# Loads of weight chunks moved from ScalarE's queue to SyncE's, and the start of their rounding tied to a count of products

## The chip, the cores and the metric

The kernel runs on one core of a Trainium2 chip. The metric is the device time of one execution in microseconds; the time before is the median of 7 runs. Engines are named as in the profile: PE (matmul), DVE (VectorE), ACT (ScalarE), POOL (GpSimd) and SP (SyncE, which here only issues DMAs). ACT can issue DMAs too.

## The reference

The output of a retention block feeds a gated feed-forward block:

```python
# q, k, v: (8, 8, 576, 64) float32, D = 64
scores = q @ k.T / sqrt(D)
ret    = scores * Dmat                 # gamma_h ** (i - j) for i >= j, else 0
x      = (ret @ v)                     # (B, H, S, D) -> (4608, 512)
xn     = x / sqrt(mean(x * x) + 1e-6) * rms_g
g, val = xn @ w_gate, xn @ w_val       # (512, 1536) each
out    = (g * sigmoid(g) * val) @ w_out  # (1536, 512)
```

The three weight matrices come as float64 and all else as float32.

## The kernel before

**Stages.** The 4608 tokens are 12 units of 384. The retention part is cut into jobs: one pair of heads of one batch (batch 1 is cut in two). Jobs 0 to 7 run first, on data loaded at the start; they give the tokens of units 0 and 1. Then come the up products of these two units (`up_plain`, line 640): for each third g of the columns, gate (m = 0) and then value (m = 1), units 0 and 1, four products each, 48 in all. A product is four matmuls of 128x384, which the trace shows as eight records; gate products are evicted by ACT (SiLU, L660), value products by DVE (L658). Jobs 8 to 11 are dealt with between these products. After that the output products of units 1 and 0 run (`across`, line 712), and then units 2 to 11 with a seven-product (Strassen) scheme for both matrices, about 950 us in which weights are already there.

**Weights.** The float64 words are rounded to float32 by the kernel. The weights are 18 chunks of 1 MB of words (lines 821 to 833): 0 to 11 for gate and value, in the order in which the up products use them, 12 to 17 for w_out. A chunk i goes through these steps:

- `load_chunk` (L855) loads its words into one of four places, `spare(i)`. A place is free when the mantissa of the chunk that was there is done. Chunks 12 to 17 have the places 1, 2, 3, 2, 3, 3; places 0 to 2 are in w_out, so chunk 17 waits for the mantissa of 16, and 16 for that of 14.
- `exponent` (DVE L871) takes the exponents out of the words; three activations on ACT (L887) turn them into scale factors. They are put in a list `acts` and issued one by one with `act()`.
- `mantissa` (DVE L898, L903, L908) makes the number without its exponent. L908 needs the last of the three activations.
- `join` (DVE L916) multiplies both.

The generator `rounding()` (line 932) puts these steps in order: exponent of i, if it was not taken ahead; exponent of i + 1, if it is loaded; mantissa of i; loads up to chunk i + 5, where a place is free; exponent of i + 1 if not yet; join of i. From chunk 4 on these loads are issued by ACT. The loop over the up products (line 1041) takes two steps of the generator behind each product (`weights(2)`), and as many as are needed at once where a product cannot go on without a chunk (`weights_to`). 

**Order.** There is no scheduler: each engine runs its instructions in the order in which the code records them, and so does each queue's issue of DMAs. An instruction that waits holds back what is behind it on its engine. Each DMA uses one of eight semaphores in turn, whichever engine issues it, and is not issued before the previous DMA with its semaphore has landed.

**Jobs among the products.** At steps 29, 33, 37 and 41 of the up products `later` calls `slot(j)` for jobs 8 to 11; at 45 the rest of job 11 follows. A slot lets PE finish the previous job (`values`, L390; `carried`, L412) and make the scores and states of this one (L307, L329); DVE weighs the scores (L342), writes x (L435, which frees the two banks of `values`) and sums the states (L366). `following(j)` then transposes job j + 1 on DVE (L272, from qraw and kraw) and scales its v on ACT (L285), and SP loads job j + 2 in 13 DMAs (qraw and kraw four each, L156; k and v two each, L224; vt, L229). The first of them waits for the transpose, since qraw has one buffer. PE has five banks of PSUM that products and slots take in turn.

After the last chunk `combine_out` (L690) makes four sums of blocks of w_out on DVE, which the output products use.

Of the kernel before, what the change touches and what calls it, by code (L numbers as in the profile page):

```python
# [35 lines left out]
def _causal_table():  # L36

    return np.ascontiguousarray(np.tile(np.triu(np.ones((L, L), np.float32)), (2, 1)))
# [3 lines left out]
def kernel(  # L42
# [11 lines left out]
    nc = tc.nc  # L54
# [776 lines left out]
    for f in range(0, NF, 2):  # L831
        chunks.append((w_out[:, f : f + 2], moe_w_out, slice(f * P, f * P + 2 * P), slice(None)))
    LATER = (1, 2, 3, 2, 3, 3)
    words_of, exp_of, waits_at = {}, {}, {}
    n_chunks = n_loads = 0

    free = w_up[0][:, 8:].rearrange("p b f -> p (b f)")
# [1 line left out]
    def spare(i):  # L839

        return i % 4 if i < n_up else LATER[i - n_up]

    def load_chunk(i, queue):
        dst, src, rws, cols = chunks[i]
        if src.dtype != F32:
            n = dst.shape[1]
            cols = slice(2 * (cols.start or 0), 2 * cols.stop if cols.stop else None)
            src = src.bitcast(U32)
            at = spare(i)
            dst = free[:, : 4 * DM] if at == 3 else (  # L850
                w_out[:, 4 * at : 4 * at + 4].rearrange("p c f -> p (c f)")
            )
            dst = words_of[i] = dst.bitcast(U32).rearrange("p (c f) -> p c f", c=n)
            waits_at[at] = i
        queue.dma_start(out=dst, in_=src[rws, cols].rearrange("(c p) f -> p c f", p=P))  # L855

    def load_chunks(n, queue=nc.scalar):

        nonlocal n_loads
        while n_loads < min(n, len(chunks)) and waits_at.get(spare(n_loads)) is None:  # L860
            load_chunk(n_loads, queue)
            n_loads += 1

    def exponent(i):

        if i not in words_of:
            return
        at = (4 + i % 2 * 2) * DM
        e = free[:, at : at + 2 * DM].bitcast(U32)
        e = e.rearrange("p (c f) -> p c f", c=chunks[i][0].shape[1])  # L870
        nc.vector.tensor_scalar(  # L871
            out=e, in0=words_of[i][..., 1::2], scalar1=20, scalar2=0x7FF,
            op0=ALU.logical_shift_right, op1=ALU.bitwise_and,
        )
        f = e.bitcast(F32)
        acts.extend((
            (i, dict(out=f, in_=e, bias=least)), (i, dict(out=f, in_=f, bias=most, scale=-1.0)),
            (i, dict(out=e, in_=f, bias=top, scale=-(2.0**23))),
        ))
        exp_of[i] = e  # L880
# [32 lines left out]
    def join(i):  # L913
        if i in words_of:
            dst = chunks[i][0]
            nc.vector.scalar_tensor_tensor(  # L916
                out=dst, in0=dst, scalar=2.0**-20, in1=exp_of.pop(i).bitcast(F32),
                op0=ALU.mult, op1=ALU.mult,
            )
            del words_of[i]  # L920
# [11 lines left out]
    def rounding():  # L932

        nonlocal n_chunks
        for i in range(len(chunks)):
            if i not in exp_of and i in words_of:
                exponent(i)
                yield
            for ahead in (True, False):
                if i + 1 in words_of and i + 1 not in exp_of and i > (1 if ahead else 0):  # L940
                    exponent(i + 1)
                    yield
                if ahead:
                    yield from mantissa(i)
                    load_chunks(i + 5 if i else 0)
                    yield
            join(i)
            n_chunks += 1
            yield
# [8 lines left out]

    def weights_to(n):

        while n_chunks < min(n, len(chunks)):
            next(steps)

    def start():

        h_of[0] = ffn.tile([P, NF, U], F32, tag="h", name="h_0")
        tables = list(zip((causal, gv, gc, gq, gx), (_causal_table(), *_decay_tables(H, D))))

        def table(i, queue):
            t, values_ = tables[i]
            src = nc.inline_tensor(values_, name=t.tensor.name + "_table")
            queue.dma_start(out=t, in_=src.ap())

        make_identity(nc, ident)
        nc.scalar.activation(out=tick, in_=mhalf[:1], func=AF.Silu)
        nc.vector.memset(ones, 1.0)
        warm = bank("warm")
        for _ in range(6):  # L980
            nc.tensor.matmul(warm[:, :P], lhsT=ones, rhs=ones, start=True, stop=True)
        first_places.update(find_places())
        load_chunks(1)
        for i in (1, 0, 2):
            table(i, nc.scalar)
        weights(3)
        for j in range(2 * NHP):
            load_first(j, {0: range(2), 1: range(2, H)}.get(j))
            if j == 1:
                table(3, nc.sync)  # L990
            load_chunks((1, 1, 1, 1, 2, 2, 2, 3)[j], nc.sync)
        table(4, nc.sync)
        nc.sync.dma_start(out=rms_g, in_=moe_rms_g.rearrange("(c p) -> p c", p=P))
        load_chunks(4, nc.sync)
        turn(0)
        scale_v(0)
        act(3)
        squares = []

        def later(step):  # L1000

            if step == LATER_AT[0] - 8:
                following(2 * NHP - 1)
            elif step in LATER_AT:
                j = 2 * NHP + LATER_AT.index(step)
                if j < LATER_JOBS:
                    slot(j, rest=(j > 2 * NHP))
                    if j + 1 < LATER_JOBS:
                        following(j)
                else:  # L1010
                    values(j - 1)
                    carried(j - 1)

        for j in range(2 * NHP):
            slot(j)
            if j + 1 < 2 * NHP:
                turn(j + 1)
            if squares:
                gather(*squares.pop())
            for i in ((1,), (2,), (3,), (4, 5), (6,), (7,), (), ())[j]:  # L1020
                scale_v(i)
            if j:
                u, c = divmod(j - 1, NHP)
                squares.append((u, c, square(u, c)))
            act(1)
            if j == 5:
                norm_1(0)
            elif j == 6:
                norm_2(0)
            weights((2, 0, 0, 1, 1, 1, 1, 0)[j])  # L1030
            if j == 4:
                gather(*squares.pop())
            elif j == 5:
                diagonals(0)
            act(1)
        gather(*squares.pop())
        load_qk(2 * NHP)
        load_kv(2 * NHP)
        made = combine_out()
        step = -1  # L1040
        for m, g in [(m, g) for g in range(NG) for m in range(2)]:
            for u in range(2):
                weights_to(4 * g + 2 * m + 1)
                for i, _ in enumerate(up_plain(u, m, g)):
                    step += 1
                    later(step)
                    if not (u or m or g):
                        if i == 0:
                            values(2 * NHP - 1)
                            carried(2 * NHP - 1)  # L1050
                            gather(1, NHP - 1, square(1, NHP - 1))
                        elif i == 1:
                            norm_1(1)
                        elif i == 2:
                            diagonals(1)
                        elif i == 3:
                            norm_2(1)
                    weights(2)
                    act(1)
                    if u and m and g == NG - 1:  # L1060
                        weights_to(len(chunks))
                        next(made, None)
                    if i == 1:
                        weights_to(4 * g + 2 * m + 2)
        for _ in made:
            pass
        for blk, t in first_blocks.items():
            keep(blk, t)
        rest = across(1)
        next(rest)  # L1070
        following(LATER_JOBS - 1)
        for i, _ in enumerate(rest):
            if i == 1:
                norm_0(2)
                differences(0)
            elif i == 2:
                norm_1(2)
                diagonals(2)
            elif i == 4:
                norm_2(2)  # L1080
        rest = across(0)
        next(rest)
        combine(1)
        slot(LATER_JOBS, rest=False)
        following(LATER_JOBS)
        for _ in rest:
            pass
        combine(0)
        slot(LATER_JOBS + 1)
        load_next(LATER_JOBS + 1)  # L1090
        turns.append(LATER_JOBS + 1)
# [74 lines left out]
```

## Time and profile before

| what | value |
|---|---|
| median of 7 runs | 1147.78 us (1145.84 to 1151.02) |
| profiled execution, its own time | 1145.84 us |
| its span, first to last instruction | 1144.1 us |
| PE busy | 1119.8 us, 98% |
| PEld busy | 1044.3 us, 91% |
| DVE busy | 733.6 us, 64% |
| ACT busy | 258.3 us, 23% |
| mean granted PE clock | 0.992 of full |
| chunks issued by ACT in the profile | w_out and w_gate places, 1024 KB each |

How to read it: a row of a timeline gives the start and duration in us, the engine (SPq and ACTq are the issuing of DMAs by SP and ACT), the line of the kernel, the operation, what it writes and reads, how many instructions are merged in the row, and in brackets how long the engine had been idle before and what ended that. The profile's lines are those of the kernel before; in the kernel after they are 3 higher from the middle of `load_chunk` on (2 higher at the load itself) and more behind `rounding`. The output products of unit 1 (`xo`, L726) start at 195.46 us.

### The profile page before, as it was taken

To read this page: it belongs to the slowest core of one execution; us is meant where nothing else is said; L and a number is where in the kernel's file an instruction comes from. 1 tells how busy PE (TensorE), PEld (TensorE's weight loads), DVE (VectorE), ACT (ScalarE), POOL (GpSimd) and SP (SyncE) were. 2 spreads that over 40 slices of the span, in tenths; PEclk is the share of its full clock that TensorE was granted. 3 is DMA by queue.
4 is the path that set the end of the run, shared out by engine and by line. 5 is a ranking of instruction groups with operands and counts; after the bars stand their busy time and mean duration, and the time that the engine had idled before them with its cause. 6 is when DMAs were issued, how large, how long until landed. Compare 5 with 4: busy or idle time off the path is not lost.

```text
span 1144.1 us, 24779 instructions
## 1 busy us (share of the span) xinstructions
PE 1119.8 (98%) x10454; PEld 1044.3 (91%) x10454; DVE 733.6 (64%) x1452; ACT 258.3 (23%) x508; POOL 40.1 (4%) x68
## 2 busy tenths in 40 slices
PE   7899988999999999999999999999999999999998
PEld 6655656999999999999999999999999999999998
DVE  5888878746686686376766676466577566446353
ACT  5556532102211221211221120121221221120210
POOL 0100000290000000000000000000000000000000
PEclk9899999999999999999999999999999999999999
DMA  8844556434553556044344456305436503303304
GB/s 209 225 130 146 143 133 193 90 68 116 125 128 68 150 139 158 8 102 106 97 117 76 110 139 130 118 27 121 103 95 140 132 32 94 128 1 98 124 1 111
DMA packets 307039, 126.72 MB, mean 111 GB/s; under 512 B 284528, under 2 KB 289904, under 8 KB 306928
## 3 DMA queue, kind: packets, MB, share of 16 engines
q1 hardware_dynamic: 296784, 108.98, 38.9%
q10 hardware_dynamic: 10144, 16.16, 4.4%
q8 instruction: 82, 1.34, 0.5%
q14 instruction: 29, 0.24, 0.1%
HBM read 110.14 MB, written 14.94 MB: 109 GB/s over the span
## 4 chain that ended last, share of the span: by engine, by line
PE 89%; DVE 6%; DMA 2%; issue 1%; ACT 1%; SPq 1%; POOL 0%; DVEq 0%; POOLq 0%; ACTq 0%
PE w L595 13%; PE x L595 12%; PE z L595 12%; PE up L652 9%; PE xo L726 8%; PE wo L726 8%; PE zo L726 8%; PE y L595 6%; PE yo L726 4%; PE av L390 2%; PE s L307 2%; PE av L412 1%; PE s L329 1%; DVE sum L366 1%; DVE x L435 1%
## 5 line engine op out<-in xcount | busy, mean ns | idle before, releaser
L619 ACT COPY m<-x 128x384 f32<-128x384 f32 x60 | 28.8, 479 | 338.0 <-PE x L595 338.0
L726 PE MATMUL xo<-h,w_out 128*128 128x192 f32 x528 | 90.3, 328 | 0.0
L595 PE MATMUL w<-sums,w_val 128*128 128x192 f32 x480 | 88.6, 328 | 0.4
L595 PE MATMUL x<-x,w_val 128*128 128x192 f32 x480 | 88.7, 328 | 0.0
L595 PE MATMUL x<-x,w_gate 128*128 128x192 f32 x480 | 88.7, 328 | 0.0
L595 PE MATMUL w<-sums,w_gate 128*128 128x192 f32 x480 | 87.9, 326 | 0.0
L595 PE MATMUL z<-x,w_gate 128*128 128x192 f32 x480 | 87.8, 326 | 0.0
L595 PE MATMUL z<-x,w_val 128*128 128x192 f32 x480 | 87.8, 326 | 0.0
L726 PEld LDWEIGHTS xo<-h,w_out 128*128 128x128 f32 x528 | 85.9, 190 | 0.6
L726 PE MATMUL wo<-h,w_out 128*128 128x192 f32 x504 | 85.6, 326 | 0.4 <-DVE c_last L774 0.4
L602 DVE TENSOR_TENSOR u<-m,y 128x384 f32<-128x384 f32 x60 | 33.1, 552 | 78.0 <-PE y L595 78.0
L726 PEld LDWEIGHTS wo<-h,w_out 128*128 128x128 f32 x504 | 82.4, 190 | 0.7 <-DVE c_last L774 0.7
L595 PEld LDWEIGHTS w<-sums,w_val 128*128 128x128 f32 x480 | 79.2, 190 | 2.7 <-DVE c L602 2.7
L595 PEld LDWEIGHTS x<-x,w_val 128*128 128x128 f32 x480 | 79.1, 190 | 0.6
L595 PEld LDWEIGHTS x<-x,w_gate 128*128 128x128 f32 x480 | 79.3, 190 | 0.5
L595 PEld LDWEIGHTS z<-x,w_gate 128*128 128x128 f32 x480 | 79.6, 190 | 0.0
L595 PEld LDWEIGHTS z<-x,w_val 128*128 128x128 f32 x480 | 79.6, 190 | 0.0
L595 PEld LDWEIGHTS w<-sums,w_gate 128*128 128x128 f32 x480 | 79.5, 190 | 0.1
L602 DVE TENSOR_TENSOR h<-u,w 128x384 f32<-128x384 f32 x60 | 33.0, 550 | 69.4 <-PE w L595 69.4
L652 PE MATMUL up<-x,w_gate 128*128 128x384 f32 x192 | 65.8, 499 | 4.8 <-DVE x L435 3.3
L614 ACT ACTIVATE h<-h 128x384 f32<-128x384 f32 x90 | 47.2, 524 | 88.5 <-DVE h L602 88.5
L652 PEld LDWEIGHTS up<-x,w_gate 128*128 128x128 f32 x192 | 36.6, 194 | 30.9 <-issue 5.6
(189 smaller groups left out, 1809.8 us busy)
## 6 DMA issues: line engine op xcount, KB each, us to landing
w_out<-w_blocks SPq DMA_DIRECT2D x70, 768.0 KB, 5.3
out_dram<-o SPq DMA_DIRECT2D x364, 24.0 KB, 1.6
qraw<-in_q_dram SPq DMA_DIRECT2D x96, 72.0 KB, 2.8
kraw<-in_k_dram SPq DMA_DIRECT2D x96, 72.0 KB, 2.8
k<-in_k_dram SPq DMA_DIRECT2D x48, 128.0 KB, 2.9
v<-in_v_dram SPq DMA_DIRECT2D x48, 128.0 KB, 3.0
w_out<-in_moe_w_gate_dram ACTq DMA_DIRECT2D x5, 1024.0 KB, 5.8
w_out<-in_moe_w_out_dram ACTq DMA_DIRECT2D x3, 1024.0 KB, 6.2
```

The costliest lines, as they stand in the source:

```text
L307: nc.tensor.matmul(s[side(odd), e, i * L : i * L + L], lhsT=d["kT"][side(e), c * L : c * L + L], rhs=d["qT"][side(e), c * L : c * L + L], ...
L329: nc.tensor.matmul(o[side(e)], lhsT=d["k"][side(odd), i, e], rhs=d["v"][side(odd), i, e], start=True, stop=True,)
L366: nc.vector.scalar_tensor_tensor(out=d["sum"][c], in0=d["sum"][c - 1], scalar=gc[:, hp : hp + 1], in1=part, op0=ALU.mult, op1=ALU.add,)
L390: mm = nc.tensor.matmul(av[odd][column(j, odd, e), i * L : i * L + L], lhsT=d["v"][side(odd), i, e] if c < NC - 1 else d["vt"][:, e], rhs= ...
L412: mm = nc.tensor.matmul(av[odd][column(j, odd, e), i * L : i * L + L], lhsT=d["sum"][c - 1][side(e)], rhs=d["qT"][side(e), c * L : c * L + L],
L435: nc.vector.tensor_tensor(out=x[to, first - c0 // L :: 2], in0=av[odd][at, i * L : (i + n) * L].rearrange("p (c k) -> p c k", k=L), in1=g. ...
L595: nc.tensor.matmul(ps[:, i * HU : i * HU + HU], lhsT=w_up[m][:, 2 * blk + c, cut], rhs=t_of[u][blk][:, c], start=(start and i == c == 0), ...
L602: nc.vector.tensor_tensor(out=o, in0=a, in1=pairs_of(ps), op=ALU.add)
L614: nc.scalar.activation(out=o, in_=c, func=AF.Silu)
L619: nc.scalar.copy(out=s1, in_=pairs_of(x_))
L652: nc.tensor.matmul(ps[:, :U], lhsT=w_up[m][:, 4 * half + c, i * P : i * P + P], rhs=x_of[u][:, c], start=(c == 0), stop=(c == NHP - 1),)
L726: nc.tensor.matmul(ps[:, i * HU : i * HU + HU], lhsT=a[:, c, i * P : i * P + P], rhs=rhs[:, c], start=(start and i == c == 0), stop=False, ...
```

## The change

`load_chunks` in `rounding()` is called with SP's queue, so chunks 4 to 17 are issued by SP, each at the place in SP's order where the code records it: among the loads of the jobs. For each chunk `there_at` holds the number of the product at which it was loaded, plus 3 (0 for chunks loaded before the up products), and `now` counts the products. `rounding()` takes the exponent of a chunk that is loaded only from that product on; while it waits so for the exponent of i itself, it gives its step back without work. Inside `weights_to` (`due`) the count is not asked for.

```diff
     LATER = (1, 2, 3, 2, 3, 3)
-    words_of, exp_of, waits_at = {}, {}, {}
+    words_of, exp_of, waits_at, there_at = {}, {}, {}, {}
+    now = 0
+    due = False
...
         queue.dma_start(out=dst, in_=src[rws, cols].rearrange("(c p) f -> p c f", p=P))
+        there_at[i] = now + 3 if now else 0
...
         for i in range(len(chunks)):
+            while i in words_of and i not in exp_of and not due and now < there_at[i]:
+                yield
             if i not in exp_of and i in words_of:
                 exponent(i)
                 yield
             for ahead in (True, False):
-                if i + 1 in words_of and i + 1 not in exp_of and i > (1 if ahead else 0):
+                if (
+                    i + 1 in words_of and i + 1 not in exp_of and i > (1 if ahead else 0)
+                    and (due or now >= there_at[i + 1])
+                ):
                     exponent(i + 1)
                     yield
                 if ahead:
                     yield from mantissa(i)
-                    load_chunks(i + 5 if i else 0)
+                    load_chunks(i + 5 if i else 0, nc.sync)
                     yield
...
     def weights_to(n):
 
+        nonlocal due
+        due = True
         while n_chunks < min(n, len(chunks)):
             next(steps)
+        due = False
...
-        step = -1
+        now = 0
...
                 for i, _ in enumerate(up_plain(u, m, g)):
-                    step += 1
-                    later(step)
+                    later(now)
+                    now += 1
```

In the order that the two kernels record on DVE, all steps of the rounding stand in the same places up to the mantissa of chunk 13 and the exponent of chunk 14. From there the exponent of 15 moves from before the mantissa of 14 to behind job 9's slot and the transposes of job 10; that of 16 from behind the join of 14 to behind the mantissa of 15; that of 17 from before the join of 16 to two products later, behind the first value product of unit 0. On SP, chunks 4 and 5 stand before job 8's loads, 6 to 12 behind them, 13 and 14 behind job 9's, 15 and 16 behind job 10's, and 17 behind the loads of both job 11 and job 12.

More of the change, by code (lines that the diff above doesn't have):

```diff
@@ L959, in weights_to @@
     def weights_to(n):
+        nonlocal due
+        due = True
         while n_chunks < min(n, len(chunks)):
             next(steps)
+        due = False
     def start():
+        nonlocal now
         h_of[0] = ffn.tile([P, NF, U], F32, tag="h", name="h_0")
```

## The prediction

> **What bounds the kernel now.** The page's busy line first, then the chain of waits in order of time, then the stages, then each engine's timeline where PE stood idle.
>
> ```profile
> span 1144.1 us, 24779 instructions
> PE 1119.8 (98%) x10454; PEld 1044.3 (91%) x10454; DVE 733.6 (64%) x1452; ACT 258.3 (23%) x508; POOL 40.1 (4%) x68
> ```
>
> PE is the bound: whatever the change is worth must be PE idle time or a slower PE clock. The stages (us, PE busy, PEld, DVE, ACT, POOL, granted clock, DMA share, GB/s) say where that is:
>
> ```profile
> 62.00:108.00 46.00, 45.29 (x142) 26.52 (x141) 41.00 (x48) 27.96 (x32) 0.00 (x0) 1.00 0.43 137
> 143.50:160.00 16.50, 13.21 (x86) 7.38 (x84) 15.22 (x24) 8.70 (x14) 0.00 (x0) 0.90 0.57 129
> 160.00:178.30 18.30, 14.69 (x198) 9.78 (x189) 10.88 (x21) 7.78 (x14) 0.18 (x2) 0.91 0.73 170
> 178.30:195.50 17.20, 16.88 (x97) 10.04 (x98) 13.31 (x23) 0.00 (x0) 0.09 (x1) 1.00 0.40 139
> ```
>
> While the up chunks are rounded (62 to 108) PE hardly stops. It loses time from 143.5 to 178.3, where the chunks of w_out are rounded, and the PE timeline names the three stops:
>
> ```profile
> 143.51 2.85 PE L652 MATMUL up<-x,w_gate 128*128 128x384 f32 x8
> 149.65 9.67 PE L652 MATMUL up<-x,w_gate 128*128 128x384 f32 x24 [3.29 <-DVE x L435]
> 174.09 0.70 PE L390 MATMUL av<-ret,v 64*64 64x64 f32 x16 [2.33 <-ACT w_val L660]
> 178.27 10.59 PE L652 MATMUL up<-x,w_val 128*128 128x384 f32 x32 [1.29 <-DVE h L658]
> ```
>
> Those are 6.9 us idle; behind the idle the clock was 0.90 and 0.91 of full, 1.65 us each. PE waits for DVE and ACT, and DVE in turn for loads:
>
> ```profile
> 144.41 0.69 DVE L871 TENSOR_SCALAR w_gate<-w_out 128x1024 uint32<-128x1024 uint32 x1 [4.67 <-DMA w_out<-in_moe_w_out_dram]
> 163.86 0.57 DVE L272 STREAM_TRANSPOSE qT<-qraw 128x384 f32<-128x384 f32 x1
> 171.78 0.69 DVE L871 TENSOR_SCALAR w_gate<-w_gate 128x1024 uint32<-128x1024 uint32 x1 [5.79 <-DMA w_gate<-in_moe_w_out_dram]
> ```
>
> The exponent of chunk 15 (144.41) and that of chunk 17 (171.78) stand in DVE's queue before their data is there, with releases of PE's banks behind them. ACT waits inside its own issue of a load, with SiLUs behind it:
>
> ```profile
> 138.04 0.40 ACTq L855 DMA_DIRECT2D w_out<-in_moe_w_out_dram  x1
> 138.50 1.15 ACT L887 ACTIVATE w_gate<-w_gate,least 128x1024 f32<-128x1024 uint32 x1 [8.27 <-DVE w_gate L908]
> ```
>
> The chain has those two loads as its longest pieces in this stretch (start, us):
>
> ```profile
> 138.04 6.26 DMA w_out<-in_moe_w_out_dram
> 166.03 5.73 DMA w_gate<-in_moe_w_out_dram
> ```
>
> **Names.** After the slot at step 33, PE runs 14 products of 2.60 us (20.80 us for eight at 94.12): A B C D, slot 37, E F G H, slot 41, I J K L, slot 45, M N, then the output products, 195.46 in the trace. From there PE has no idle time that the change touches, so the whole gain is how much earlier than 195.46 they start.
>
> **Up to 134 us: nothing.** DVE's built order is the same through the rounding of chunk 13 and the exponent of chunk 14, so the three-product rule binds nowhere before. ACT loses 14 issues (0.37 to 0.40 us each, 5.4 us of an engine that is busy 23%); SP gains 14. Chunks 4 and 5 now stand in front of job 8's loads, which start at 50.7 instead of 48.09; these are transposed at 108.61, which covers it. Chunk 13 stands behind job 9's loads (SP done 117.6): issued 117.6 instead of 115.21, landed about 122.9, its exponent ran at 123.45. If that cover failed, DVE has 0.5 us of waiting for PE just behind it. Earlier exponents on ACT only shorten DVE's waits on ACT, under a PE that never stops.
>
> **Chunk 14 to 16: the two stops at 149.65 and 174.09.** I replay the new order with durations of the trace, start to start: L871 0.61, L898 0.72, L903 1.14, L908 1.25, L916 1.14, L887 1.1, L658 0.5, a slot's DVE work 3.65 up to its first transpose and 0.96 for the two.
> - ACT no longer sits on chunk 15's issue: the exponent of 14 ran on DVE at 129.75, so its three L887 end by 140.9 (the first SiLU of this round, free at 139.3, between them).
> - DVE, free at 139.66, does not wait for chunk 15: mantissa of 14 139.66 to 142.75, join to 143.9, slot 33's work to 148.1. Its L435 release banks by 145.1 and 145.7 (149.5 before): A, B, C, D run without a stop, 143.51 to 153.9.
> - SP: job 10's loads start at 134.15. Its second v load waited 3.5 us for ACT's chunk 15 (the two share a DMA semaphore); that wait goes. 13 issues at the usual 7.0 to 7.9 us end at 142.0, chunk 15 follows, 4.0 us later than on ACT. Landing about 147.4; its exponent is now due at 148.1. Chunk 16 follows at 142.8 (148.13 before), landed by about 151, due at 153.9.
> - Exponent 15 148.1; ACT's three with SiLUs A and B between end 152.7; mantissa 15 ends 153.95, exponent 16, join 15, mantissa 16's first two to 157.5. Slot 37 is on PE by 155.6; E waits for SiLU C behind exponent 16 on ACT, 156.2 (0.6 idle); H ends at 166.6 (171.43 before). DVE's slot work follows at 157.5, the first transpose ends at 161.3 (164.43 before), mantissa 16 ends 162.95, join and L658 of G by 164.8.
>
> **Chunk 17: the new stop.** On ACT it left right behind mantissa 16 (166.03). On SP it stands behind the 13 loads of job 12, whose first waits for that transpose (161.3). A later job of this width shows the price:
>
> ```profile
> 261.83 1.95 SPq L156 DMA_DIRECT2D qraw<-in_q_dram  x4
> 263.88 2.06 SPq L156 DMA_DIRECT2D kraw<-in_k_dram  x4
> 265.98 1.05 SPq L224 DMA_DIRECT2D k<-in_k_dram  x2
> 267.14 0.99 SPq L224 DMA_DIRECT2D v<-in_v_dram  x2
> 268.24 0.61 SPq L229 DMA_DIRECT2D vt<-in_v_dram  x1
> ```
>
> 7.0 us; so chunk 17 leaves at 168.4. How long it then takes, on SP behind 13 small loads, no row shows. A chunk alone took 4.9 to 5.2, on ACT beside a job's loads 5.7 to 6.3, on SP behind the first loads 5.45 (at 38.04) and 8.4 (at 24.51, everything in flight). I take 5.5, nearest to the 38.04 case, ends 4.9 and 8.4: landed 173.9.
>
> Behind exponent 17 DVE holds L898, the L658 of H, slot 41's L342 and L435. PE runs slot 41 (1.7) and I, to 170.9; J needs the bank that the L658 of H frees: 173.9 + 0.61 + 0.72 + 0.55 = 175.8. That is 4.9 us idle, and the clock falls behind it: I take 1.5 us (1.65 in each earlier stage), ends 0.7 and 2.4. Then J K L 7.8, slot 45 1.4, M N 5.2: output products at 175.8 + 7.8 + 1.5 + 1.4 + 5.2 = 191.7. Mantissa and join of 17 end at 183; L690 and L710 have 12 us to the second output product.
>
> **Sum.** 195.46 - 191.7 = 3.7 us less. The profiled execution took 1145.84 us (span 1144.1 and 1.7 around it) and becomes 1142.1; it is the lowest of the seven, 1.9 under their median 1147.78, which becomes 1144.1.
>
> [...]
>
> **Rivals.**
> 1. *SP jams* (ends slower). Two jobs beside chunk loads held SP 11.2 (134.15 to 145.35) and 10.0 us (164.46 to 174.42). If SP is as slow again, chunk 15 leaves at 145.4, lands at 150.8, 2.7 late; chunk 17 leaves at 174.0, lands at 179.5, J at 181.4, output products 197.3: 1.8 us more; with 6.3 flights 3.5 more, 1151.3. It turns to a loss when chunk 17 lands past 177.6. Against it: the 3.5 in the first goes with the shared semaphore, and the slow k issues of the second had chunk 17 in flight beside them.
> 2. *The stop only moves* (no change). Issue 8.1 us, as for the jobs at 201 and 231, and a 6.3 flight: landed 175.8, output products 193.6, 1.9 us less: 1145.9.
> 3. *Short stop.* Flight 4.9, clock 0.7: 190.3, 5.2 less: 1142.6.
> 4. *The rule does nothing.* It moves three exponents only; without it DVE would still stand at 15. The order shows that it moves, so I give this no share.
>
> **Chances.** 0.2% is 2.3 us, about what a measurement here can tell from no change. Forecast and rival 3 together 0.58, rival 2 0.25, rival 1 0.17, of which 0.15 beyond 0.2%. Faster 0.58, same 0.27, slower 0.15. The likeliest case alone spans 1142.5 to 1145.5. For 8 in 10 I go from 1140 (rival 3 and the lower half of the spread of seven runs) to 1150 (rival 1 with 5.5 flights, 1149.6).
>
> **What would show it.** After: no PE stop near 146 to 150 and none by ACT's L660 in slot 41; no ACT issue of a chunk but the first; L871 of chunk 15 without a DMA wait; L871 of chunk 17 waiting some 9 us (164.8 to 173.9), then one PE stop near 5 us released by DVE's L658; output products near 191.7. Wrong if chunk 15 lands after 148.1 (each us then delays everything to chunk 17), if SP needs over 9 us for job 12, or if PE stops before 134.

## The result and the profile after

| | before | after |
|---|---|---|
| median | 1147.47 us (38 runs, 1145.52 to 1151.02) | 1144.32 us (16 runs, 1142.62 to 1145.67) |
| profiled execution, its own time | 1145.84 us | 1142.3 us |
| span | 1144.1 us | 1140.5 us |

The ratio is 0.9969, 95% interval 0.9962 to 0.9976: 3.6 us faster (2.8 to 4.4); the two medians in the table differ by 3.2 us. That is a small gain; the experiments show that it is the difference of two opposed effects, each larger than it. In what follows, "below before" and "over before" are (ratio - 1) x the median of before.

The page of the kernel after, its first lines:

```profile
span 1140.5 us, 24777 instructions
PE 1117.6 (98%) x10454; PEld 1042.1 (91%) x10454; DVE 733.0 (64%) x1452; ACT 258.5 (23%) x508; POOL 40.5 (4%) x68
```

The same stages as before (start:end in us, length, busy time and instructions of PE, PEld, DVE, ACT and POOL, granted PE clock, DMA share, GB/s):

```profile
62.00:108.00 46.00, 46.00 (x143) 27.18 (x144) 41.38 (x48) 26.39 (x30) 0.00 (x0) 1.00 0.44 139
143.50:160.00 16.50, 16.23 (x146) 9.98 (x145) 14.08 (x31) 9.69 (x16) 0.09 (x1) 1.00 0.56 168
160.00:178.30 18.30, 13.04 (x131) 7.81 (x130) 8.09 (x18) 4.58 (x7) 0.09 (x1) 0.92 0.68 164
178.30:195.50 17.20, 16.88 (x109) 11.47 (x108) 15.85 (x19) 0.63 (x2) 0.09 (x1) 0.99 0.59 217
```

The stage from 143.5 us has lost its stop and its slow clock (16.23 us busy of 16.5, where before had 13.21 at 0.90). The next one is worse than before: 13.04 of 18.3 us. Rows of PE's timeline show the one long stop that is in it:

```profile
142.42 10.59 PE L652 MATMUL up<-x,w_gate 128*128 128x384 f32 x32
154.94 5.43 PE L652 MATMUL up<-x,w_gate 128*128 128x384 f32 x16 [0.27 <-ACT w_val L660]
175.23 9.69 PE L652 MATMUL up<-x,w_val 128*128 128x384 f32 x24 [5.26 <-DVE h L658]
191.52 4.06 PE L726 MATMUL xo<-w_val,w_out 128*128 128x192 f32 x24
```

Products A to D run in one piece, E waits 0.27 us, and J waits 5.26 us for DVE. DVE's timeline shows for what:

```profile
147.04 0.65 DVE L874 TENSOR_SCALAR w_gate<-w_out 128x1024 uint32<-128x1024 uint32 x1
162.99 0.55 DVE L658 TENSOR_TENSOR h<-h,up 128x384 f32<-128x384 f32 x1
173.41 0.69 DVE L874 TENSOR_SCALAR w_gate<-w_gate 128x1024 uint32<-128x1024 uint32 x1 [9.88 <-DMA w_gate<-in_moe_w_out_dram]
174.02 0.69 DVE L901 TENSOR_SCALAR w_out<-w_gate 128x1024 uint32<-128x1024 uint32 x1
174.63 0.55 DVE L658 TENSOR_TENSOR h<-h,up 128x384 f32<-128x384 f32 x1
```

The exponent of chunk 15 (147.04) finds its data there. The exponent of chunk 17 waits 9.88 us for its load, and the L658 that frees J's bank (174.63) stands two instructions behind it. In the chain of waits the load starts only when the issues in front of it are through (the last rows before J):

```profile
159.49 0.58 DVE qT L272
160.09 0.34 SPq L156
...
166.51 0.61 SPq L229
...
167.22 6.17 DMA w_gate<-in_moe_w_out_dram
173.41 0.69 DVE w_gate L874
```

The gain is the stops of before that went, with the slow clock behind them (0.90 and 0.91 in their stages), less the new one with its half-rate clock (0.50 for 3.43 us, 0.92 in its stage).

### The profile page after: what moved, and what is told of

It reads as the page before. It is cut to its first block, busy times and chain, and to the rows that moved or that the text cites. A ratio compares the mean times of both kernels' runs of the same rounds, so it can differ in the third digit from the quotient of the medians.

```text
span 1140.5 us, 24777 instructions
## 1 busy us (share of the span) xinstructions
PE 1117.6 (98%) x10454; PEld 1042.1 (91%) x10454; DVE 733.0 (64%) x1452; ACT 258.5 (23%) x508; POOL 40.5 (4%) x68
## 4 chain that ended last, share of the span: by engine, by line
PE 89%; DVE 5%; DMA 2%; issue 1%; SPq 1%; ACT 1%; POOL 0%; DVEq 0%; POOLq 0%; ACTq 0%
PE w L595 13%; PE x L595 13%; PE z L595 13%; PE xo L726 8%; PE wo L726 8%; PE zo L726 8%; PE up L652 8%; PE y L595 6%; PE yo L726 4%; PE av L390 2%; PE s L307 1%; PE av L412 1%; PE s L329 1%; DVE sum L366 1%; DVE x L435 1%
## 5 line engine op out<-in xcount | busy, mean ns | idle before, releaser
L652 PE MATMUL up<-x,w_val 128*128 128x384 f32 x192 | 65.2, 498 | 5.3 <-DVE h L658 5.3
```

Of the source, the lines that this page charges most:

```text
L652: nc.tensor.matmul(ps[:, :U], lhsT=w_up[m][:, 4 * half + c, i * P : i * P + P], rhs=x_of[u][:, c], start=(c == 0), stop=(c == NHP - 1),)
```

## The experiments

The theory is that of the prediction: SP's queue relieves ACT, the rule keeps DVE from waiting at chunks that are not there, and chunk 17 alone loses, because 13 issues of job 12 stand in front of it on SP. Rivals: one half of the change does everything; chunk 17 is late by its flight among other traffic and not by the issues; the rule's delay is what costs.

### Each half alone

Chunks still issued by ACT, the rule kept:

```diff
-                    load_chunks(i + 5 if i else 0, nc.sync)
+                    load_chunks(i + 5 if i else 0)
```

> The three-product rule alone; all chunks from 4 on are issued by ACT, as in the kernel before. My theory: the gain is all in the place of the exponents, and SP's part costs. Replayed on the trace after: mantissa 13 ends at 136.9 and chunk 15 leaves ACT there, in time for its exponent at 147.9; ACT holds some SiLUs (about 0.8 us), chunk 17 leaves at 162.5 right behind mantissa 16, lands by 168.6, J starts at 170.6 without a stop, output products at 185.0 instead of 191.5: about 1137.8 us, 9 to 10 us (0.8%) under the kernel before. Rival: the gain of the change comes from ACT's freedom to issue SiLUs (the queue's move); then the rule alone stays near the kernel before, within 2 us of 1147.5, and keeps stops by ACT's L660 near 174.

Measured 1138.83 us, ratio 0.9925 (0.9906 to 0.9945): 8.6 us below before, and faster than both halves together. The stop before J is gone but for 0.4 us, and a stop before E has come, 2.36 us where 0.8 was expected. PE's timeline of this kernel:

```profile
160.14 5.43 PE L652 MATMUL up<-x,w_gate 128*128 128x384 f32 x16 [2.36 <-ACT w_val L660]
172.34 11.00 PE L652 MATMUL up<-x,w_val 128*128 128x384 f32 x32
```

ACT's timeline of the same kernel says why E is late:

```profile
146.33 0.39 ACTq L857 DMA_DIRECT2D w_gate<-in_moe_w_out_dram  x1
146.77 0.49 ACT L660 ACTIVATE h<-up 128x384 f32<-128x384 f32 x1 [3.17 <-issue]
147.83 0.46 ACT L285 ACTIVATE v<-v,gv 128x192 f32<-128x192 f32 x1 [0.57 <-DMA v<-in_v_dram]
152.10 0.35 ACT L285 ACTIVATE vt<-vt,gv 64x64 f32<-64x64 f32 x1 [3.82 <-DMA vt<-in_v_dram]
```

The issue of chunk 16 holds a SiLU for 3.17 us, and behind it ACT waits 3.82 us for job 10's vt, with the scale factors of chunk 15 behind that. SP issued this vt late, at 146.63, and beside chunk 16, so that it landed at 152.08: the v load in front of it went out only at 146.22, as it uses the semaphore of ACT's chunk 15, which landed at 146.20. The chain of waits has these pieces:

```profile
139.44 6.77 DMA w_out<-in_moe_w_out_dram
146.22 0.37 SPq L224
146.63 5.45 DMA vt<-in_v_dram
```

So chunks on ACT hold ACT directly, and through the eight shared semaphores SP too (the 895 DMAs of the trace of before use eight, 111 or 112 each; there, too, job 10's second v load went out at 144.33, behind the landing of ACT's chunk 15 with the same semaphore at 144.31). It works the other way as well: mantissa 14, which frees chunk 16's place, ended at 144.86, and chunk 16 went out only at 146.33, when a kraw load of job 10 with the same semaphore had landed (146.26).

All chunks on SP, the rule taken out:

```diff
-        there_at[i] = now + 3 if now else 0
+        there_at[i] = 0
```

> The move to SP alone, exponents in the places of the kernel before (the product count is never asked for). My theory: exponent 15 again stands on DVE before mantissa 14 and waits for a load that leaves 4 us later than on ACT (141.1), until 146.4; slot 33's DVE work ends 8 us later than in the trace after, job 12's loads start at 166.0, chunk 17 leaves at 173.1 and lands at 179.3, with the join of 16 and the L658 of G behind it: I starts at 185.2, output products at 203.9: about 1156.7 us, 9 us (0.8%) over the kernel before. Rival (ACT's freedom is the gain): faster than the kernel before by 2 us or more. Rival (the queue does not matter, small issue time): within 2 us of the kernel before.

Measured 1155.24 us, ratio 1.0071 (1.0056 to 1.0086): 8.1 us slower than before. DVE waited 7.6 us at the exponent of chunk 15 and 11.8 us at that of 17:

```profile
146.86 0.69 DVE L874 TENSOR_SCALAR w_gate<-w_out 128x1024 uint32<-128x1024 uint32 x1 [7.62 <-DMA w_out<-in_moe_w_out_dram]
179.79 0.69 DVE L874 TENSOR_SCALAR w_gate<-w_gate 128x1024 uint32<-128x1024 uint32 x1 [11.78 <-DMA w_gate<-in_moe_w_out_dram]
```

PE's timeline:

```profile
149.17 9.42 PE L652 MATMUL up<-x,w_gate 128*128 128x384 f32 x24 [3.31 <-ACT h L660]
182.10 0.70 PE L390 MATMUL av<-ret,v 64*64 64x64 f32 x16 [11.07 <-ACT w_val L660]
186.27 12.22 PE L652 MATMUL up<-x,w_val 128*128 128x384 f32 x32 [1.28 <-DVE h L658]
```

What follows: the gain is the rule's, and the move of the loads takes part of it back. The rule is worth 8.6 us with ACT's loads and 11.7 us with SP's (8.1 + 3.6); moving the loads costs 8.1 us without the rule and 5.0 us with it. That it still costs 5.0 is what the next three runs take apart.

### Chunk 17's place in the queue

Chunk 17 on SP, but issued in front of job 12's loads: the step behind slot 37 that recorded these loads leaves them out, and they are recorded behind product G, where chunk 17 has been issued. (That is three products later; the text of the expectation says four.)

```diff
-                    if j + 1 < LATER_JOBS:
+                    if j == LATER_JOBS - 2:
+                        prepare_next(j)
+                    elif j + 1 < LATER_JOBS:
...
+                    if now == LATER_AT[2] + 4:
+                        load_next(LATER_JOBS - 2)
```

> The changed kernel with one thing moved: the loads of job 12 are recorded four products later, so that chunk 17 stands before them on SP. My theory: the one stop left (5.3 us before J, and the slow clock behind it) is the 13 issues in front of chunk 17. It leaves at 161.7, lands at 166.8, exponent 17 runs at once, L658 of H ends at 168.5, J follows I at 169.7 with no stop, output products at 184.1: 7.4 us less than the changed kernel, about 1136.9 us. Rival (the load of the chunk itself is what is late, its flight grows when it stands before the 13 loads): less than 3 us gained. Rival (the next wait, the rounding on DVE and ACT, sets J): 3 to 5 us.

Measured 1136.59 us, ratio 0.9905 (0.9890 to 0.9919). PE's timeline has no stop at J (the row at 169.17 is I, with J, K, L behind it in one piece):

```profile
156.99 5.43 PE L652 MATMUL up<-x,w_gate 128*128 128x384 f32 x16 [0.26 <-ACT w_val L660]
169.17 10.59 PE L652 MATMUL up<-x,w_val 128*128 128x384 f32 x32
```

Chunk 17 issued by ACT, all others by SP:

```diff
-                    load_chunks(i + 5 if i else 0, nc.sync)
+                    load_chunks(i + 5 if i else 0, nc.scalar if i == 16 else nc.sync)
```

> Chunk 17 alone is issued by ScalarE, all others by SP. Theory: it leaves with job 12's first loads, at about 161.5 on the changed kernel's scale, takes 6.2 to 6.6 us beside them, lands near 168, TensorE doesn't stop before J, and the end comes 7 to 8 us earlier: 1136.5 to 1137.5 us. Rival (an issue on ScalarE holds the SiLU that stands behind it wherever it is put): a stop of 2 us or more before one of the products E to H and 1139 us or more.

Measured 1136.26 us, ratio 0.9903 (0.9888 to 0.9917). The rival fell. ACT does hold SiLUs here, 3.59 us, but PE does not notice: its only stop from A to J is the 0.27 us before E:

```profile
154.49 5.43 PE L652 MATMUL up<-x,w_gate 128*128 128x384 f32 x16 [0.27 <-ACT w_val L660]
166.69 10.59 PE L652 MATMUL up<-x,w_val 128*128 128x384 f32 x32
```

With chunk 17 early on either engine, then, the gain is 10.9 to 11.1 us, where the rule alone had 8.6. That the other chunks on SP are worth the 2.3 to 2.5 us between them is likely, not certain: in the traces E's wait falls from 2.36 to 0.26 us, but the intervals touch (0.9906 to 0.9945, against 0.9890 to 0.9919 and 0.9888 to 0.9917).

The dose: eight more issues in front of chunk 17, with the same bytes. The loads of job 12's raw q and k are cut in two:

```diff
-                    nc.sync.dma_start(out=t[r : r + SQ, c0 * L // SQ :], in_=rows[i])
+                    a, z = c0 * L // SQ, S // SQ
+                    cuts = (a, z // 2, z) if j == 3 * NHP else (a, z)
+                    for a, z in zip(cuts, cuts[1:]):
+                        n = a - c0 * L // SQ
+                        nc.sync.dma_start(out=t[r : r + SQ, a:z], in_=rows[i][:, n : n + z - a])
```

> Job 12's loads of raw q and k are split in two each, so SP issues 21 DMAs instead of 13 in front of chunk 17, with the same bytes. Theory (chunk 17 is late by the time that SP takes to issue what stands in front of it): 8 more issues at about 0.53 us (7.0 us for 13 in the changed kernel) put its issue 4.2 us later, 171.4 against 167.2 in time from a start like that one's, and product J, the output products and the end by as much, with up to 0.5 us of half-rate clock: about 1148.5 us. Rival (chunk 17 is late by its flight beside job 12's traffic, or J waits for another thing): the same bytes, so less than 1.5 us, at most 1145.8.

Measured 1147.78 us, ratio 1.000 (0.999 to 1.001): the gain is gone. SP's queue in this kernel (its lines are 4 higher):

```profile
162.52 3.81 SPq L160 DMA_DIRECT2D qraw<-in_q_dram  x8
166.43 3.89 SPq L160 DMA_DIRECT2D kraw<-in_k_dram  x8
170.37 1.01 SPq L228 DMA_DIRECT2D k<-in_k_dram  x2
171.48 0.99 SPq L228 DMA_DIRECT2D v<-in_v_dram  x2
172.58 0.61 SPq L233 DMA_DIRECT2D vt<-in_v_dram  x1
173.29 0.54 SPq L861 DMA_DIRECT2D w_gate<-in_moe_w_out_dram  x1
```

From the first issue to chunk 17 are 10.8 us, against 7.1 in the kernel after: 3.6 us for eight issues, 0.46 each (0.53 was expected). PE's stop at J grows by the same 3.65 us:

```profile
181.32 9.62 PE L656 MATMUL up<-x,w_val 128*128 128x384 f32 x24 [8.91 <-DVE h L662]
197.54 4.06 PE L730 MATMUL xo<-w_val,w_out 128*128 128x192 f32 x24
```

All times counted from the start of product A, so that the beginning of the run drops out (us; issue and landing are those of chunk 17's DMA):

| kernel | chunk 17 issued | landed | stop before J | output products |
|---|---|---|---|---|
| chunk 17 ahead of job 12 | 19.23 | 24.83 | none | 41.88 |
| chunk 17 alone on ACT | 19.24 | 25.27 | none | 41.91 |
| rule alone (all on ACT) | 21.94 | 28.58 | 0.4 | 45.02 |
| after | 24.80 | 30.97 | 5.26 | 49.10 |
| 21 issues in front | 28.45 | 34.64 | 8.91 | 52.70 |

J starts 1.84 us behind the landing where it waits (32.81 after, 36.48 with 21 issues), and would start at 27.3 if it didn't wait (in the kernel of the first row I starts at 24.69, and a product takes 2.6). So chunk 17 is early enough if it lands by 25.46 on this scale. The two kernels without a stop make that by 0.6 and 0.2 us. The row of the rule alone agrees: landing plus 1.84 is 30.4, and there J was due at 30.05, being held up at E already; its row of four products is 11.00 us instead of 10.59.

That settles it: with its place changed, chunk 17 costs nothing; with eight more issues in front, the end moves by what these issues take. The flight plays a small part: 6.17 us after and 6.19 with 21 issues, 5.60 in the first row, so that of the 6.1 us by which chunk 17 lands earlier there 5.6 are its issue.

### Which exponents the rule has to move

The rule for chunk 15 alone:

```diff
-        there_at[i] = now + 3 if now else 0
+        there_at[i] = now + 3 if now and i == 15 else 0
```

> The rule of three products for chunk 15's exponent alone; 16 and 17 begin theirs where the kernel before did. Theory (with SP's late chunk 17 each exponent that is put early holds VectorE's product behind it until its chunk is there): exponent 15 no longer stops TensorE before E, so no stop of 3.3 us near 150; exponent 17 waits until chunk 17 lands, near 173.4, with the product of G behind it, TensorE stops before I for 5 to 8 us, and the output products begin 6 us later than in the changed kernel: about 1150.5 us, between the two. Rival (exponent 15 is all that the rule is worth): no more than 1 us over the changed kernel, 1145.3 or less.

Measured 1152.19 us, ratio 1.0042 (1.0026 to 1.0059). Between SP alone and the whole change, as the theory had it, though 1.7 us above its number. PE's timeline:

```profile
156.60 5.43 PE L652 MATMUL up<-x,w_gate 128*128 128x384 f32 x16
177.85 0.71 PE L390 MATMUL av<-ret,v 64*64 64x64 f32 x16 [10.41 <-ACT w_val L660]
182.03 10.59 PE L652 MATMUL up<-x,w_val 128*128 128x384 f32 x32 [1.28 <-DVE h L658]
```

The stop of chunk 15 is gone, but chunk 17's is 11.7 us and in another place than expected: not before I, but in slot 41, behind a SiLU. ACT's timeline has it:

```profile
176.28 1.15 ACT L890 ACTIVATE w_gate<-w_gate,least 128x1024 f32<-128x1024 uint32 x1 [16.43 <-DVE w_gate L874]
177.33 0.47 ACT L660 ACTIVATE w_val<-up 128x384 f32<-128x384 f32 x1
```

An early exponent puts its scale factors early into ACT's queue as well, ahead of the SiLUs of E and F, and both engines wait for the one load, DVE 11.92 us and, behind it, ACT 16.43. That the rule counts products keeps it out of both queues.

The exponent of chunk 17 two products later still, the rest as after:

```diff
-        there_at[i] = now + 3 if now else 0
+        there_at[i] = now + (5 if i == 17 else 3) if now else 0
```

> The changed kernel with the count for chunk 17 alone at five products instead of three: its load is where it was (lands near 173.4), its exponent stands on DVE behind the L658 of I. My theory: J to N no longer wait for it, output products of unit 1 start at 184.2, but join 17 ends at 180.6 and the four L690 and the L710 behind it end at 191.6, so the second output product (195.4 in the trace after) waits on DVE until then: 3 to 4 us less than the changed kernel, 1140.5 to 1142. Rival (the load itself is waited for wherever it is needed, so its place on DVE does not matter): within 1 us of 1144.3. Rival (only the bank behind H mattered): 7 us less.

Measured 1141.48 us, ratio 0.9952 (0.9936 to 0.9969). J no longer stops, and the output products start at 41.88 on the scale of the table, but the second of them waits:

```profile
184.60 4.06 PE L726 MATMUL xo<-w_val,w_out 128*128 128x192 f32 x24
191.94 5.82 PE L726 MATMUL zo<-t,w_gate 128*128 128x192 f32 x24 [3.27 <-issue]
```

The profile names no releaser for this wait ("issue"). But the product reads t, and until 191.84, 0.1 us before it starts, DVE is busy with the sums of w_out's blocks (L690) and then of the activations (L710, which writes t), all pushed back by the late chunk 17. On the scale of the table PE's stop moved by 16.4 us (from J at 32.81 to 49.22) and is 2 us shorter. The cause is the load, and a later exponent only chooses who waits for it.

### The first stage

Chunk 17 ahead of job 12 as above, and chunks 4 to 11 on ACT again:

```diff
-                    load_chunks(i + 5 if i else 0, nc.sync)
+                    load_chunks(i + 5 if i else 0, nc.scalar if i < 8 else nc.sync)
```

> The kernel with chunk 17 ahead of job 12, and chunks 4 to 11 issued by ScalarE again; 12 to 17 by SP. Theory (SP's issue of the chunks before 130 us changes nothing that TensorE waits for): within 1 us of that kernel's 1136.6 us. Rival (they hold ScalarE in the first stage as later ones do near 155): 2 us or more slower, 1138.6 or more.

Measured 1135.73 us, ratio 0.9898 (0.9883 to 0.9912), which cannot be told from 0.9905 (0.9890 to 0.9919) of the kernel with these chunks on SP. Within these intervals, some 1.7 us to each side, who issues the first chunks makes no difference; the effect is that of chunks 12 to 17. This kernel, and those with chunk 17 moved, are faster than before and after. All three have no stop over 0.4 us of PE between A and the output products, so no more than that is left to win there by removing waits.

## Why the prediction was right

**The size.** The profiled execution was to take 1142.1 us and took 1142.3; the median was to be 1144.1 and was 1144.32. The stretch that the prediction worked out, from A to the output products, came out 0.9 us longer than predicted (49.1, against 48.2), and the start of the run 1.1 us shorter than in the trace of before, which the prediction had put down as nothing: the agreement to 0.2 us has that luck in it. In the stretch itself the gain is 2.85 us (51.95 before, 49.10 after), not 3.7.

**The two stops that go.** Confirmed: no stop from A to D, E's wait 0.27 (0.6 predicted), exponent 15 without a wait at 4.62 us behind A (4.6 predicted). But the prediction puts this down to both parts of the change, and did not price the rule by itself. The halves show that the rule alone takes away the stops before B and in slot 41 (a wait of 2.36 us before E comes instead) and is 5.0 us faster than the whole, while SP alone keeps both stops (3.31 and 11.07 us). One duration in the replay is written wrongly: DVE's work in a slot takes 3.25 us up to its first transpose (148.01 to 151.26 before, 142.83 to 146.08 after), not 3.65; the sums go by 3.25.

**Chunk 17.** Job 12's first load was to go out 17.8 us behind A and did at 17.7; chunk 17 at 24.9, and did at 24.8. The term furthest off is the flight: 5.5 us taken, 6.17 measured, inside the ends 4.9 and 8.4. Chunk 17 took 6.2 to 6.6 us in all five kernels where it left right behind job 12's loads (after, SP alone, 21 issues, the rule for 15 alone, exponent 17 later), so the price of a chunk beside a job's loads (5.7 to 6.3 before) was nearer. What lengthened it is not isolated: after, the last of these loads landed 2.0 us behind chunk 17's issue (169.21), and SP issued a store of 768 KB (w_blocks, L676) right behind it, at 167.82. The longer flight moved J by 0.5 us (32.8 instead of 32.3). The clock behind the stop took 1.7 us (J to the output products 16.29, against 14.56 where there is no stop), 1.5 predicted.

The granted clock in the stretch around J, in windows of the kernel after:

```profile
169.96:175.22 5.26, 0.01 (x1) 0.00 (x0) 1.81 (x4) 1.08 (x1) 0.00 (x0) 1.00 0.90 304
175.22:178.65 3.43, 3.42 (x6) 1.91 (x7) 3.23 (x11) 3.37 (x7) 0.00 (x0) 0.50 0.02 5
178.65:184.90 6.25, 6.25 (x24) 3.45 (x23) 6.24 (x7) 0.28 (x2) 0.00 (x0) 1.00 0.23 77
```

Half rate for 3.43 us behind the stop, which is 1.7 us lost; the stop that the prediction priced at 4.9 + 1.5 cost 5.26 + 1.7.

**The rivals.** SP did not jam: once no chunk was in flight beside job 12's loads, their 13 issues took 7.0 us. The slow k issues of before came back where chunk 17 was in flight beside them: in the kernel with chunk 17 ahead of job 12 the eight issues of raw q and k took 6.2 us instead of 4.1. "The stop only moves" was half true: it moved, and was smaller. The rival that the rule does nothing was right to get no share: without it the same queue costs 11.7 us more.

**The issues in front.** The prediction priced the 13 issues in front of chunk 17 at 7.0 us. One issue is small beside the load, 0.55 of 6.17 us. But chunk 17 stood behind 13 of them, which took 7.1 us from the first to its own, more than the load itself; with them out of the way the gain is 10.9 us (0.9905).

## What to carry to other kernels

The load moved to SP's queue went out at 167.22, when the last of the 13 issues recorded in front of it was through (167.12), and the first of those had waited for a transpose until 160.09: read the trigger and the count of DMAs in front, here 13 at some 0.5 us, before pricing the flight. Put a late, urgent load ahead of a batch of loads that are needed later; here this one reordering was worth twice the change itself. And keep instructions that wait for a load out of the queues that free buffers for the bounding engine until the load can have landed (here that was worth 11.7 us with the loads on SP); where the load itself was late, deferring its exponent further moved the stop by 16.4 us and took 2 us off it.

## What was not expected of the hardware

- The same idle time does not always cost clock. The stop of 2.33 us before 174.09 in the trace of before went with a clock of 0.50 from 173.79 to 177.20; the stop of 2.36 us before 160.14 in the kernel with the rule alone was followed by 1.00 from 160 to 178.3 us. In the trace with 21 issues the clock was 0.80 over the stop of 8.91 us and 0.52 in the 3.42 us behind it. Up to the output products the half-rate stretches of the trace of before start at 9.95, 33.84, 44.08, 149.89 and 173.79; each lasts 3.41 us, and their starts are 7, 3, 31 and 7 such lengths apart. What decided between the two stops of one length is not shown.
- Product A starts at different times in kernels that are the same up to it: 141.97 (chunk 17 on ACT), 142.42 (after), 142.72 (exponent 17 later), 144.42 (rule for chunk 15), 144.48 (chunk 17 ahead of job 12), 144.84 us (21 issues). In the three early ones the granted clock in the first 20 us was 0.83; in the three late ones it was 1.00 there and 0.91 in the 20 us behind that (which one of the early ones, exponent 17 later, had as well). So it may go with where the half-rate stretches fall in the loading phase; this is a coincidence of six traces and was not tried. The kernel with the rule alone, whose loads ACT issues, had 0.83 and A at 144.92, so it does not hold for every kernel. The six starts spread over 2.9 us, nearly as much as the change is worth, so comparisons inside the span are better made from a common event than from its start.
